# A spectral mixer with a feed-forward layer on one core: transfers of the prologue begun by another engine, weight stores and some loads at other steps

## The chip, the core and the metric

The kernel runs on one core of one Trainium2 chip. The time is the device time of one execution in microseconds; three runs of the kernel before have a median of 2681.63 us. TensorE does matmuls, ScalarE (ACT) copies, casts and activations, VectorE (DVE) and GpSimd (POOL) elementwise work, and SyncE (SP) begins transfers. Each engine works through its own instructions in order, so a waiting instruction holds all that stand behind it on that engine.

## The reference

For each of 8 sequences `x` of 3072 tokens by 256 channels: a real Fourier transform along the sequence, a complex matmul of each frequency with `w_r`, `w_i` (256 x 256), a bias, soft shrinkage by 0.01, and the inverse transform. Then a feed-forward layer on all 24576 tokens: `h = x @ w_in` (256 to 2048), softplus, `@ w_out` (2048 to 256). In short:

```
X = rfft(x, axis=1)
Yr = Xr @ w_r - Xi @ w_i + b_r ;  Yi = Xr @ w_i + Xi @ w_r + b_i
Y = sign(Y) * max(|Y| - 0.01, 0)         (for both parts)
out = softplus(irfft(Y) @ w_in) @ w_out
```

Inputs and output are float32.

## The kernel before

The transform of a sequence is done in stages of small dense matmuls, with 3072 = 96 x 32. `s1` multiplies 16 chunks of x by a 96 x 96 matrix and gives `a`; `s3` does the second factor on 12 pairs of groups (`ap` tiles, with their matrix `g1`); `mix` multiplies by `w_r` and `w_i`, adds the bias and shrinks; `s4` gives `d`; `s5` gives the 512-token blocks of the layer's input (`dp` tiles of d, with their matrix `hm`). From a stage to the next the partitions change, so `a` and `d` are written to DRAM (`a_dr`, `d_dr`) and read back; for the first sequence (b = 0) `a` stays in `a0` in SBUF and `ap` is copied from there (line 273). The `d` loads of a sequence wait until all 12 stores of `d` have landed.

The feed-forward layer takes tokens in pairs of 512 and the hidden units in 8 blocks of 256, with a seven-product scheme for a block (`slot_products`, banks "c" and "e" of PSUM). Matmuls are done in split precision: an operand becomes a high and a low part, and `mm3` (lines 207 to 210) does three matmuls. The layer's weights come as 64-bit floats. `split_w` (line 146) takes one block through a chain of ScalarE, VectorE and GpSimd work, one part a step, to a tile `w` of high and low parts, which is stored to DRAM (line 195, `w_dr`). The main loop reads the blocks back with `stream_w` (line 200), 896 KB for a block of `w_in` and 512 KB for one of `w_out`, two buffers each. The tile `w` is `w_1` for `w_in` blocks of the prologue, else `wp`, which has one buffer (line 168). Blocks are started three steps apart after the prologue; in a block's third part VectorE writes `w` for the first time (L178 or L182), in its fourth ScalarE makes the high half (L192), in its fifth VectorE the low half (L194).

The order of the work is written out by hand. A step has a number; steps below 0 are the prologue (`t0` = -66), each key of the main loop (a pair of 512-token blocks and one hidden block) has four. In a step come, in this order: the feed-forward products of the step, the due parts of `split_w` (the dictionary `before`), at most one product of the transform (`steps`), the loads and splits asked for at this step (`fill`, in the order in which they were asked for), what was put off in the step before (`later`, stores of `a` and `d` among it), and the second half of the feed-forward work. Each engine gets its instructions in this order. `early` is a list that is emptied at step -1; up to there it tells the prologue. In the prologue `s1` uses four tiles of `a1` in turn for `a` of b = 1 (line 257), and `d` has two.

All transfers of the prologue but a few constants are begun by SP: x (line 231), the weights as they come (line 143), `g1` (line 749, `g1_0` for b = 0), `ap` (line 273), stores of `a` and `d` (line 100), stores of weights (line 195), their loads (line 204), `hm` and `dp` (lines 440, 441). `plan_s1` (line 645) asks for x of chunk c seven steps before its product. For the chunks 10 to 15 of b = 1 x has two buffers (line 230), so a load of x c waits for the split of x c-2.

Of the kernel before, what the change touches and what calls it, by code (L numbers as in the profile page):

```python
# [10 lines left out]
F32 = mybir.dt.float32  # L11
# [8 lines left out]
NG = 24  # L20
# [13 lines left out]
def tile_spectral_mixer_mlp(ctx, tc, x, w_r, w_i, bias, bias_0, w_in, w_out, f, f_hi, f_lo, g1, g3, g3_hi, g3_lo, hm, out):  # L34
# [12 lines left out]
    nc = tc.nc  # L47
# [21 lines left out]
    a0 = sb.tile([P, N2 * D], F32, tag="y0", name="a0", bufs=1)[:N1].rearrange("p (n c) -> p n c", n=N2)  # L69
# [5 lines left out]
    w1_dr = [dram.tile([P, 2 * 7 * P], F32, name=f"w1_dr{m2}", tag=f"w1_dr{m2}", bufs=1) for m2 in range(NM // 2)]  # L75
    w2_dr = [dram.tile([P, 2 * 2 * D], F32, name=f"w2_dr{m2}", tag=f"w2_dr{m2}", bufs=1) for m2 in range(NM // 2)]
# [19 lines left out]

    def store(dst, src, what):

        def start():
            nc.sync.dma_start(dst, src)  # L100
            stored[what] += 1

        later.append(start)
# [42 lines left out]
    def split_w(which, m2):  # L146

        st = stages.pop((which, m2)).bitcast(U32).rearrange("p (n w) -> p n w", w=2)
        lw, hw = st[:, :, 0], st[:, :, 1]
        t = sb.tile([P, 512], F32, tag="t", name="wt", bufs=5)
        u = sb.tile([P, 512], F32, tag="ot", name="wu")
        ti, ui = t.bitcast(U32), u.bitcast(U32)
        v, g = nc.vector, nc.gpsimd
        nc.scalar.activation(u, hw.bitcast(F32), AF.Square)
        v.tensor_scalar(out=ti, in0=hw, scalar1=3, scalar2=0x3FFFFFF8, op0=ALU.logical_shift_left, op1=ALU.bitwise_and)
        v.scalar_tensor_tensor(out=ti, in0=hw, scalar=0xC0000000, in1=ti, op0=ALU.bitwise_and, op1=ALU.bitwise_or)  # L160
        nc.scalar.mul(lw.bitcast(F32), lw, 2.0 ** -52)
        yield
        v.scalar_tensor_tensor(out=t, in0=u, scalar=2.0 ** -30, in1=t, op0=ALU.is_ge, op1=ALU.mult)
        v.tensor_scalar(out=ui, in0=ti, scalar1=0xFF800000, scalar2=None, op0=ALU.bitwise_and)
        g.tensor_tensor(out=u, in0=lw.bitcast(F32), in1=u, op=ALU.mult)
        yield
        n = 7 * P if which else 2 * D
        w = w_1 if early and which else sb.tile([P, 2 * 7 * P], F32R, tag="wp", name="wp", bufs=1)
        w = w[:, :2 * n]
        hi, lo, src = w[:, :n], w[:, n:], w[:, n:].bitcast(F32)  # L170
        ahead = bool(early)
        e = g if ahead else v
        if which:

            tm, um = [a.rearrange("p (k m n) -> p m k n", k=2, m=2) for a in (t, u)]
            a21 = tm[:, 1, 0]
            o = [src[:, i * P:(i + 1) * P] for i in range(7)]
            e.tensor_tensor(out=src[:, A11 * P:(A11 + 2) * P].rearrange("p (k n) -> p k n", k=2), in0=tm[:, 0], in1=um[:, 0], op=ALU.add)  # L178
            e.tensor_tensor(out=a21, in0=a21, in1=um[:, 1, 0], op=ALU.add)
            e.tensor_tensor(out=o[A22], in0=tm[:, 1, 1], in1=um[:, 1, 1], op=ALU.add)  # L180
        else:
            e.tensor_tensor(out=src, in0=t, in1=u, op=ALU.add)  # L182
        if ahead:
            yield
            yield
        if which:
            v.tensor_tensor(out=o[S1], in0=a21, in1=o[A22], op=ALU.add)
            v.tensor_tensor(out=o[S3], in0=o[A11], in1=a21, op=ALU.subtract)
            v.tensor_tensor(out=o[S2], in0=o[S1], in1=o[A11], op=ALU.subtract)
            v.tensor_tensor(out=o[S4], in0=o[A12], in1=o[S2], op=ALU.subtract)  # L190
        yield
        nc.scalar.copy(hi, src)  # L192
        yield
        v.tensor_tensor(out=lo, in0=src, in1=hi.bitcast(F32), op=ALU.subtract)  # L194
        nc.sync.dma_start((w1_dr if which else w2_dr)[m2][:, :], w.bitcast(F32))
        stored["w", which, m2] += 1

    w_t = {}
# [22 lines left out]
    early = [None]  # L221
# [44 lines left out]
    def load_a(b, gp):  # L266
        assert stored["a", b] == 16
        t = sb.tile([P, 512 + 2 * P], F32, tag="ap", name="ap", bufs=3)
        t, g1_t = t[:, :512].rearrange("p (g c) -> p g c", g=2), t[:, 512:].rearrange("p (g n) -> p g n", g=2)
        if b == 0:  # L270
            g1_t = g1_0[:, 2 * gp:2 * gp + 2]
            for g in range(2):
                nc.sync.dma_start(t[:, g, :], a0[2 * gp + g::NG])
        else:
            nc.sync.dma_start(g1_t, g1[:, 2 * gp:2 * gp + 2])
            nc.sync.dma_start(t, a_dr[b][8 * gp:8 * gp + 8].rearrange("(g q) n c -> (q n) g c", g=2))
        a_sb[b, gp] = t, g1_t
# [301 lines left out]
    def slot_products(s, key, prev):  # L579

        if s == 0:
            if key:
                ffn1(key, "c", A11, B11)
                ffn1(key, "e", A12, B21)
                snap(key, C11, "c")
            if prev:
                softplus(prev, C21)
                high(prev, C21)
                low(prev, C12)
            if key:  # L590
                add(key, C11, "e")
            if prev:
                low(prev, C21)
        elif s == 1 and key:
            ffn1(key, "c", S2, T2, start=False)
            ffn1(key, "e", S3, T3)
            softplus(key, C11)
            high(key, C11)
            snap(key, C21, "c")
            low(key, C11)  # L600
        elif s == 2 and key:
            ffn1(key, "c", S1, T1, start=False)
            snap(key, C22, "c")
            add(key, C22, "e")
        elif s == 3 and key:
            ffn1(key, "c", S4, B22, start=False)
            ffn1(key, "e", A22, T4, start=False)
            softplus(key, C22)
            high(key, C22)
            softplus(key, C12, "c")  # L610
            high(key, C12)
            low(key, C22)
            add(key, C21, "e")

    def slot_second(s, key, prev):
        if s < 3:
            if prev:
                what = (C22, C12, C21)[s]
                ffn2(prev, what, what == C22 and prev[2] == 0, what != C22 and prev[2] == NM // 2 - 1)
                if s == 2:  # L620
                    del w_t[0, prev]
        elif key:
            ffn2(key, C11, key[2] == 0, False)
            del w_t[1, key]


    with tc.manual_schedule():
# [3 lines left out]
        fill, steps, before = {}, {}, {}  # L631
# [3 lines left out]
        def at(i, f, *args):  # L635
            fill.setdefault(int(i), []).append((f, args))

        def product(i, f, *args):
            i = int(i)
            while i in steps:  # L640
                i += 1
            steps[i] = f, args
            return i

        def plan_s1(b, start, step, first=0):
            for c in range(first, 16):
                t = product(start + step * (c - first), s1, b, c)
                at(t - 3, split_x, b, c)
                at(t - 7, load_x, b, c)

        def plan_mix(b, start, step):
            mixed = done = start
# [29 lines left out]
        t0 = -len(first)  # L682
        for t, (what, b, i) in enumerate(first, t0):
# [9 lines left out]
                product(t, s4, b, i)  # L693
            else:
                product(t, s5, 0, b, i)
        for t, i, j in ((t0 + 15, 0, 4), (t0 + 16, 4, 12), (t0 + 22, 12, NG)):
            at(t, nc.sync.dma_start, g1_0[:, i:j], g1[:, i:j])
        at(t0 + 18, nc.sync.dma_start, bias0, bias_0)
        at(-6, nc.sync.dma_start, bias_sb, bias)
# [3 lines left out]
        for j in range(NM):  # L703
            t = t0 + 23 + 5 * j if j < 9 else 1 + 3 * (j - 9)
            at(t - (6 if j < 9 else 4 if j < 12 else 2), load_w, (j + 1) % 2, j // 2)
            before.setdefault(t, []).append(split_w((j + 1) % 2, j // 2))
# [9 lines left out]

        nt = NT
        plan_s1(1, 1, 1.6, 10)
        for b in range(B):
            for bp in range(1, NPAIR):  # L720
# [15 lines left out]
        for i in range(min([*fill, *steps]), nt * B + 3):  # L736
            due = len(later)
            if i >= 0:
                g, s = divmod(i, 4)
                key, prev = keys[g], keys[g - 1] if g else None  # L740
                slot_products(s, key, prev)
            for part in before.pop(i, ()):
                if next(part, part) is None:
                    before.setdefault(i + 1, []).append(part)
            if i in steps:
                f, args = steps.pop(i)
                f(*args)
            for f, args in fill.pop(i, ()):
                f(*args)
            for _ in range(due):  # L750
                later.popleft()()
            if i >= 0:
                slot_second(s, key, prev)
# [101 lines left out]
```

## Time and profile before

| | us |
|---|---|
| median of three runs | 2681.63 |
| lowest and highest run | 2677.0, 2682.29 |
| span of the profiled execution | 2678.0 |
| TensorE busy in it | 2603.8 (97%) |
| VectorE busy | 1626.2 (61%) |
| ScalarE busy | 1719.5 (64%) |
| GpSimd busy | 301.3 (11%) |

The page gives the span of the profiled execution, from its first to its last instruction, and no time around it; the median of the runs is 3.6 us above this span. Busy time is an average over stages: the table says that TensorE is nearly full over the whole, and not where it waits. That is read from windows and timelines of the first 250 us, in which the prologue and the conversion of the weights lie.

### The profile page before, as it was taken

Reading aid. Unit: us, or ns where it says so; the run is one execution under the profiler, and the core shown is the slowest. Engines: PE = TensorE matmul, PEld = TensorE weight load, DVE = VectorE, ACT = ScalarE, POOL = GpSimd, SP = SyncE. Lnnn points to the kernel's source line nnn. Section 1 sums busy time; section 2 is a strip of 40 time slices with the busy share of each in tenths; the row PEclk is TensorE's granted clock in tenths of the full one; section 3 lists DMA queues with packets and bytes.
Section 4 is the critical chain, followed back from the end, with each engine's and each line's share of the span. In section 5 each row is a group of like instructions: output and inputs, shape, how many; then the busy total and the mean of one; then the engine's idle time right before and its main releaser. Section 6 shows DMA issues by size and latency. Waiting matters only on the chain.

```text
span 2678.0 us, 36264 instructions
## 1 busy us (share of the span) xinstructions
PE 2603.8 (97%) x13059; PEld 2184.2 (82%) x13059; DVE 1626.2 (61%) x2701; ACT 1719.5 (64%) x3115; POOL 301.3 (11%) x292
## 2 busy tenths in 40 slices
PE   7768999999999999999999999999999999999999
PEld 5546888888888888888888888888888888888887
DVE  3666665666646666566665666556665666645454
ACT  3365666666666666666676666666666666666665
POOL 2432110110101101101011011010010000000000
PEclk8889999999999999999999999999999999999999
DMA  6766556556455565564555644646455455445543
GB/s 191 254 210 206 194 164 198 166 187 193 157 188 178 178 198 170 179 205 156 184 172 172 217 159 153 220 163 198 164 167 191 155 170 188 142 154 183 186 147 110
DMA packets 186116, 479.73 MB, mean 179 GB/s; under 512 B 18097, under 2 KB 86961, under 8 KB 185937
## 3 DMA queue, kind: packets, MB, share of 16 engines
q1 hardware_dynamic: 185376, 476.95, 55.1%
q8 instruction: 103, 1.69, 0.3%
q0 software_dynamic: 560, 0.47, 0.1%
q14 instruction: 77, 0.62, 0.1%
HBM read 390.31 MB, written 83.89 MB: 177 GB/s over the span
## 4 chain that ended last, share of the span: by engine, by line
PE 88%; DVE 2%; DMA 2%; ACT 1%; issue 0%; POOL 0%; SPq 0%; DVEq 0%; ACTq 0%; POOLq 0%
PE pso L208 13%; PE pso L209 12%; PE pso L210 12%; PE psc L208 6%; PE psc L210 6%; PE psc L209 6%; PE pse L208 5%; PE pse L210 5%; PE pse L209 5%; PE psf L455 4%; PE psf L209 4%; PE psf L208 4%; PE psf L210 4%; PE psf L287 2%; DMA w_dr<-wp 1%; DVE shrunk L413 0%
## 5 line engine op out<-in xcount | busy, mean ns | idle before, releaser
L553 DVE TENSOR_TENSOR gl<-t,gh 128x512 fp32r<-128x512 f32 x768 | 533.2, 694 | 349.7 <-ACT gh L547 346.8
L532 ACT COPY t<-psc 128x512 f32<-128x512 f32 x576 | 337.0, 585 | 504.4 <-PE psc L210 502.4
L537 DVE TENSOR_TENSOR t<-pse,t 128x512 f32<-128x512 f32 x576 | 396.2, 688 | 426.9 <-ACT t L532 278.3
L208 PE MATMUL pso<-gh,w 128*128 128x512 f32 x1536 | 616.2, 401 | 0.0
L209 PE MATMUL pso<-gl,w 128*128 128x512 f32 x1536 | 600.0, 391 | 0.0
L210 PE MATMUL pso<-gh,w 128*128 128x512 f32 x1536 | 599.5, 390 | 0.0
L547 ACT CAST gh<-t 128x512 fp32r<-128x512 f32 x768 | 476.8, 621 | 58.2 <-PE pso L210 34.4
L543 ACT ACTIVATE t<-t 128x512 f32<-128x512 f32 x576 | 364.5, 633 | 58.7 <-DVE t L537 58.0
L210 PEld LDWEIGHTS pso<-gh,w 128*128 128x128 f32 x1536 | 288.7, 188 | 62.5
L208 PEld LDWEIGHTS pso<-gh,w 128*128 128x128 f32 x1536 | 290.1, 189 | 54.9
L209 PEld LDWEIGHTS pso<-gl,w 128*128 128x128 f32 x1536 | 290.0, 189 | 51.4
L208 PE MATMUL psc<-y_sb,w 128*128 128x512 f32 x768 | 301.6, 393 | 16.1 <-DMA w<-w_dr 7.8
L210 PE MATMUL psc<-y_sb,w 128*128 128x512 f32 x768 | 300.1, 391 | 0.0
L209 PE MATMUL psc<-y_sb,w 128*128 128x512 f32 x768 | 299.6, 390 | 0.0
L208 PE MATMUL pse<-y_sb,w 128*128 128x512 f32 x576 | 227.8, 396 | 14.4 <-DVE t L537 7.9
L115 POOL TENSOR_TENSOR xl<-xt,xh 96x512 fp32r<-96x512 f32 x102 | 134.1, 1317 | 938.3 <-ACT xh L106 783.6
L209 PE MATMUL pse<-y_sb,w 128*128 128x512 f32 x576 | 225.2, 391 | 0.0
L210 PE MATMUL pse<-y_sb,w 128*128 128x512 f32 x576 | 225.1, 391 | 0.0
L489 POOL TENSOR_TENSOR y_sb<-raw,y_sb 128x512 fp32r<-128x512 f32 x69 | 92.3, 1337 | 1128.5 <-ACT y_sb L486 1124.9
L208 PEld LDWEIGHTS psc<-y_sb,w 128*128 128x128 f32 x768 | 144.5, 188 | 51.0 <-ACT t L532 10.2
L210 PEld LDWEIGHTS psc<-y_sb,w 128*128 128x128 f32 x768 | 144.6, 188 | 31.0
L209 PEld LDWEIGHTS psc<-y_sb,w 128*128 128x128 f32 x768 | 144.6, 188 | 29.7
(131 smaller groups left out, 3637.8 us busy)
## 6 DMA issues: line engine op xcount, KB each, us to landing
w<-w_dr SPq DMA_DIRECT2D x192, 896.0 KB
w<-w_dr SPq DMA_DIRECT2D x192, 512.0 KB
dp<-d_dr SPq DMA_DIRECT2D x80, 384.0 KB
xt<-in_x SPq DMA_DIRECT2D x128, 192.0 KB
d_dr<-d SPq DMA_DIRECT2D x96, 256.0 KB
out_y<-ot SPq DMA_DIRECT2D x96, 256.0 KB
ap<-a_dr SPq DMA_DIRECT2D x84, 256.0 KB
a_dr<-a SPq DMA_DIRECT2D x102, 192.0 KB
```

Source lines behind the costliest of these rows:

```text
L115: (eng or nc.vector).tensor_tensor(out=lo, in0=src, in1=hi.bitcast(F32), op=ALU.subtract)
L208: nc.tensor.matmul(ps, wh, xh, start=start, stop=False, skip_group_check=more)
L209: nc.tensor.matmul(ps, wh, xl, start=False, stop=False, skip_group_check=more)
L210: nc.tensor.matmul(ps, wl, xh, start=False, stop=stop, skip_group_check=more)
L287: nc.tensor.matmul(xv[:, g, k], t[:, g, k * P:(k + 1) * P], g1_t[:, g].rearrange("p (c s) -> p c s", c=2), start=True, stop=True,)
L455: nc.tensor.matmul(ps[:, t - blk * BLK:t - blk * BLK + n], d_sb[b, blk // 2, n2 // 4][0][:, n2 % 4, k * P:(k + 1) * P], d_sb[b, blk // 2, ...
L489: eng.tensor_tensor(out=lo, in0=raw[j], in1=hi.bitcast(F32), op=ALU.subtract)
L532: nc.scalar.copy(t, banks[bank])
L537: nc.vector.tensor_tensor(out=t, in0=banks[bank], in1=t, op=ALU.add)
L543: nc.scalar.activation(t, banks[bank] if bank else t, AF.Softplus)
L547: nc.scalar.copy(gh, ct[key, what])
L553: nc.vector.tensor_tensor(out=gl, in0=ct.pop((key, what)), in1=gh.bitcast(F32), op=ALU.subtract)
```

## The change

Six edits. While `early` is not empty, stores of `a` and `d` are begun by ScalarE. Weight stores come one step later than the low half, and blocks whose third part lies in the prologue (`ahead`) are stored by ScalarE. The first three pairs of `ap` of b = 0 (six transfers) are begun by ScalarE. The loads of x for b = 1, chunks 10 to 15, are asked for five steps ahead of the product and not seven. The first part of `g1_0` is asked for at `t0 + 9` and not at `t0 + 15`. Where several weight blocks have a part in the same step, those under way now come ahead of one that starts in it, in their old order; before, they were appended behind it.

```diff
@@ store
+        queue = nc.scalar if early else nc.sync
+
         def start():
-            nc.sync.dma_start(dst, src)
+            queue.dma_start(dst, src)
             stored[what] += 1
@@ split_w
         v.tensor_tensor(out=lo, in0=src, in1=hi.bitcast(F32), op=ALU.subtract)
-        nc.sync.dma_start((w1_dr if which else w2_dr)[m2][:, :], w.bitcast(F32))
+        yield
+        (nc.scalar if ahead else nc.sync).dma_start((w1_dr if which else w2_dr)[m2][:, :], w.bitcast(F32))
@@ load_a
             for g in range(2):
-                nc.sync.dma_start(t[:, g, :], a0[2 * gp + g::NG])
+                (nc.scalar if gp < 3 else nc.sync).dma_start(t[:, g, :], a0[2 * gp + g::NG])
@@ plan_s1
                 at(t - 3, split_x, b, c)
-                at(t - 7, load_x, b, c)
+                at(t - (5 if b == 1 else 7), load_x, b, c)
@@ the plan of the prologue
-        for t, i, j in ((t0 + 15, 0, 4), (t0 + 16, 4, 12), (t0 + 22, 12, NG)):
+        for t, i, j in ((t0 + 9, 0, 4), (t0 + 16, 4, 12), (t0 + 22, 12, NG)):
             at(t, nc.sync.dma_start, g1_0[:, i:j], g1[:, i:j])
@@ the loop over steps
-            for part in before.pop(i, ()):
-                if next(part, part) is None:
-                    before.setdefault(i + 1, []).append(part)
+            left = [part for part in before.pop(i, ()) if next(part, part) is None]
+            if left:
+                before[i + 1] = left + before.get(i + 1, [])
```

## Rows read from the trace of the kernel before

**Rows 1.** Windows: us, busy us (and count) of five engines, TensorE clock, DMA share, GB/s.
```profile
75.00:108.00 33.00, 26.70 (x156) 20.84 (x157) 28.98 (x43) 12.01 (x24) 19.62 (x15) 0.94 0.79 263
108.00:125.00 17.00, 10.37 (x31) 6.19 (x29) 4.13 (x9) 4.37 (x8) 6.37 (x8) 0.70 1.00 289
200.00:250.00 50.00, 38.23 (x180) 31.46 (x181) 30.20 (x56) 24.49 (x46) 10.42 (x13) 0.90 0.65 211
400.00:600.00 200.00, 199.21 (x1021) 168.46 (x1019) 121.06 (x202) 134.44 (x245) 25.34 (x27) 1.00 0.59 186
...
205.00:225.00 20.00, 14.87 (x63) 11.35 (x61) 8.03 (x14) 7.15 (x13) 5.08 (x11) 0.91 1.02 314
```

**Rows 2.** Timeline of TensorE: start, duration, line, tiles; in brackets idle before and releaser.
```profile
27.83 2.53 PE L287 MATMUL psf<-y,ap 128*128 128x128 f32 x8 [4.25 <-DMA ap<-a]
...
43.41 0.58 PE L210 MATMUL psf<-wmh,w 128*128 128x256 f32 x1 [4.77 <-DVE w L115]
...
119.88 1.99 PE L455 MATMUL psf<-dp 96*128 96x96 f32 x8 [5.95 <-DMA dp<-d_dr]
...
139.20 0.79 PE L208 MATMUL pse<-y_sb,w 128*128 128x512 f32 x1 [6.50 <-ACT y_sb L474]
...
157.72 0.77 PE L208 MATMUL psc<-y_sb,w 128*128 128x512 f32 x1 [7.14 <-DMA w<-w_dr]
```

**Rows 3.** Timeline of SP's queue; two answers have the starts at 20.84.
```profile
20.84 7.17 SPq L273 DMA_DIRECT2D ap<-a  x6
...
20.84 1.34 SPq L273 DMA_DIRECT2D ap<-a  x2
...
118.11 1.33 SPq L100 DMA_DIRECT2D a_dr<-y  x2
...
143.02 0.31 SPq L231 DMA_DIRECT2D xt<-in_x  x1
...
152.77 0.42 SPq L204 DMA_DIRECT2D w<-w_dr  x1
...
193.02 0.33 SPq L195 DMA_DIRECT2D w_dr<-wp  x1
194.15 0.39 SPq L143 DMA_DIRECT2D w<-in_w_out  x1
...
203.89 0.32 SPq L195 DMA_DIRECT2D w_dr<-wp  x1
205.04 0.38 SPq L143 DMA_DIRECT2D w<-in_w_in  x1
```

**Rows 4.** Timeline of ScalarE, its copies of a, w and y_sb.
```profile
21.90 0.58 ACT L260 COPY y<-psf 96x512 f32<-96x512 f32 x1 [0.28 <-PE psf L249]
...
30.40 0.58 ACT L301 CAST w<-psf 128x512 fp32r<-128x512 f32 x1 [4.74 <-PE psf L287]
...
108.25 0.58 ACT L260 COPY y<-psf 96x512 f32<-96x512 f32 x1
...
125.88 0.58 ACT L260 COPY y<-psf 96x512 f32<-96x512 f32 x1 [12.38 <-DMA a_dr<-y]
...
138.57 0.57 ACT L474 CAST y_sb<-psf 128x512 fp32r<-128x512 f32 x1
```

**Rows 5.** Timeline of VectorE.
```profile
41.52 0.69 DVE L380 TENSOR_TENSOR z<-psf,bias 128x512 f32<-128x512 f32 x1 [9.19 <-DMA bias<-in_bias]
...
195.85 0.43 DVE L178 TENSOR_TENSOR wp<-wt,wu 128x256 f32<-128x256 f32 x1
...
201.07 0.69 DVE L537 TENSOR_TENSOR t<-pse,t 128x512 f32<-128x512 f32 x1 [1.68 <-ACT t L532]
...
207.85 0.69 DVE L182 TENSOR_TENSOR wp<-wt,wu 128x512 f32<-128x512 f32 x1 [1.70 <-DMA w_dr<-wp]
...
214.07 0.69 DVE L553 TENSOR_TENSOR gl<-t,gh 128x512 fp32r<-128x512 f32 x1 [2.21 <-ACT gh L547]
...
225.40 0.42 DVE L178 TENSOR_TENSOR wp<-wt,wu 128x256 f32<-128x256 f32 x1 [8.37 <-DMA w_dr<-wp]
```

## The prediction, made before the changed kernel ran

> **What bounds the kernel now.** I read the windows first. From 400 us on TensorE works 199.2 of 200 us [rows 1]: whatever the change does there is covered by matmuls. It works 26.7 of 33 us from 75 to 108, 10.4 of 17 from 108 to 125 and 38.2 of 50 from 200 to 250 [rows 1]. All edits fall before step 24, so the prologue (below 141 us) and the 25 steps after it (to 250 us) decide. Then TensorE's timeline says what each gap waits for [rows 2]: 4.25 us for the first ap, 4.77 for VectorE's low half, 5.95 for dp, 6.50 for a copy on ScalarE, 7.14 for the first weights of the second pass over the hidden blocks. The queues of SP, ScalarE and VectorE [rows 3 to 5] tell why.
>
> **Loads of x at other steps (b = 1), and with them the 7.14 us.** A tile of x c is free when c-2 has been split. Before, x14 stands in step 0 ahead of the weight load, and SP waits for x12's split of step 2; only at 152.77 the load starts that TensorE gets at 157.72 [rows 2, 3]. Now x14 is in step 2 and x13 in step 0; x13 was begun at 143.02 [rows 3]. The load can start about 143.5 and, with the same 4.95 us to its use (157.72 - 152.77), is there at 148.4. TensorE would want it at 157.72 - 7.14 = 150.58. The stall goes, -7.1 us; what is late next is VectorE. At worst it uses the gap to catch up and takes 2 us of it back, so -5.1 to -7.1. The other x are still there a step before their split: cost 0.
>
> **Stores of a on ScalarE's queue, and with them the 6.50 us.** In steps 56 to 61 four a tiles take turns. The fifth copy waits for the first store's landing and runs at 125.88, after 12.38 us idle [rows 4]. On SP that store stands behind the d loads, which wait for all stores of d: it started at 118.11 [rows 3], though its copy ran at 108.25 [rows 4]. ScalarE is in order, so its copy of B21 came at 138.57 [rows 4] and TensorE's matmul at 139.20 [rows 2]. Now ScalarE begins the store itself, a step (some 2 us) after the copy, about 111; with the 7.8 us that it took (118.11 to 125.88) it lands at 119, and the copy runs 7 us earlier. What is late next is TensorE's own s5, which ends about 131. I take the whole 6.50: -6.5. SP is also held no more by weight stores, so it asks for the weight loads of steps 53 to 57 (1.9 MB) before the last d stores rather than beside them, and the 5.95 us for dp could shrink too: up to -12.4. But a stores now run beside the d loads, and in this stretch the DMA share is 1.00 [rows 1]: if these lose what the copies gain, 0.
>
> The Trainium skill (DMA: Bandwidth & Descriptors, section "Issuing engines are not separate DMA queues") speaks against this edit: transfers started by any engine run on the same 16 DMA engines and interleave, and starting them elsewhere saves only the time on the sequencer. The share of 1.00 [rows 1] agrees; the 12.38 us of rows 4 are, however, a wait of SP's order and not of the engines. By the rule alone this term would be 0 and the sum 6.5 us higher; it is the second rival's ground.
>
> **First six ap and the prologue's other starts on ScalarE.** On SP six starts of ap took 7.17 us, 1.2 each [rows 3]. ScalarE reaches them after the second b = 1 copy (21.90 + 0.58 = 22.5 [rows 4]), 1.7 us later than SP at 20.84; but SP's queue ahead of them is shorter by the first g1 load, now six steps earlier. I leave the 4.25 us as they are (-1 to +2). Behind them ScalarE has three a starts at 0.67 (118.11: two in 1.33 [rows 3]), two copies and two casts at some 0.6 each, then the copy of 30.40 [rows 4]. At the pace of SP's first two ap, 0.67 each (two in 1.34 [rows 3]), 22.5 + 4.0 + 2.0 + 2.4 = 30.9, a loss of 0.5; at 1.2, 34.1, of 3.7. The gain: VectorE waited 9.19 us for the bias until 41.52 [rows 5], which stood on SP behind eight ap and an a store; that gave the 4.77 us. It still stands behind the fourth ap pair, and one us of the 4.77 stays (the low half comes after z in VectorE's order). I take -1.0 with that loss in it, from +3.7 to -3.8. The later ap loads and d copies, less held by SP, gain 0: from 75 to 108 VectorE works 29.0 of 33 us and sets the pace [rows 1] (its 4.0 idle are the most that can go). The d and weight starts cost ScalarE 0.3 to 0.7 us each [rows 3], beside 12.0 us of work in those 33 and 4.4 in the 17 after [rows 1]: 0.
>
> **Weight stores a step later.** This is the term that costs. wp has one buffer: the next weight's first write (VectorE L178 or L182, two steps after its start, starts three steps apart) waits for the store's landing. Before, the store went out in the step of its low half, ahead of that step's loads; now it stands behind them, in the step of the next write. What the row shows when such a store lands late: VectorE stood 8.37 us at 225.40 [rows 5]. Stores in order after step 0:
> - w_out 4, step 5 to 6: nothing between. w_in 5, 8 to 9: two loads, whose buffers TensorE frees a step before the low half is ready. w_in 7, 20 to 21: the same. 0 each.
> - w_out 5, 11 to 12: before at 193.02, landed by 195.85 (no wait there) [rows 3, 5]: 0.52 MB in 2.8 us; at 314 GB/s [rows 1] 1.7 of it are data, 1.2 the rest. Now the stage load is ahead (before at 194.15; it waits for GpSimd, whose input VectorE now makes after the low half, +0.7, so 194.8), an ap load of 0.39 MB and a weight load of 0.52. With these, 1.97 MB at 314 GB/s are 6.3 us: landed at 194.8 + 6.3 + 1.2 = 202.3, a wait of 6.5. VectorE had 1.68 us idle behind it at 201.07 [rows 5]: +4.8.
> - w_in 6, 14 to 15: before at 203.89, the write waited 1.70 at 207.85 [rows 3, 5]. Now behind the stage load (before at 205.04; + 0.7 + 4.8 = 210.5) and four d chunks with their hm: 2.69 MB, and 0.92 of its own, 3.6 MB, 11.5 us at the full rate of this stretch (share 1.02 [rows 1]). Landed at 223.2; the write is ready at 207.85 - 1.70 + 4.8 = 210.95: a wait of 12.3, 10.6 more; less the 2.21 idle at 214.07 [rows 5], +8.4.
> - w_out 6, 17 to 18: it waited 8.37 before, since those same loads were ahead; now they are gone and one load and one ap are ahead: 0.
>
> Together +13.2. Bounds: 0, if VectorE is not what the PE waits for there (TensorE ran 38.2 of 50 us [rows 1], so some slack is there), and 18.8 without any slack.
>
> **The sum.** -7.1 - 6.5 - 1.0 + 13.2 = -1.4 us. The profiled span is 2678.0; the page gives no time around it, and the median of three runs, 2681.63, lies 3.6 above, 0.14%. So 2676.6 of span, 2680 measured. From 250 us on nothing gives it back: TensorE is full [rows 1].
>
> **The rivals.** (1) Faster: the late stores bind less. For it: at 195.85 VectorE did not wait at all, and TensorE can run ffn blocks ahead of VectorE there. Against: 8.37 us at 225.40 show that it stands when a store is late, and the share is 1.02. With only 3 of the 13.2: 2678.0 - 11.6 = 2666.4, measured 2670. It decides if the two waits together stay under 5 us.
> (2) Slower: ScalarE, now a queue of its own in front of its copies. Place: 22 to 36 and 108 to 125 us. Price: the 3.7 us of the ap starts, no 6.5 and no 1.0. It decides once a start on ScalarE takes 1.2 us rather than 0.67, or an a store beside the d loads lands later than 126. Then -7.1 + 13.2 + 3.7 = +9.8: 2691. For it: 1.2 each on SP, the share of 1.00. Against: ScalarE's queue begins empty. By the rule named above, with starts at 0.67, it would be -1.4 + 6.5 = +5.1, measured 2687.
> (3) The edits cancel because the same transfers end at the same times: 2682.
>
> **How the numbers follow.** 0.2%, 5.4 us, is what a measurement of this kernel can tell: 2676.3 to 2687.0 counts as the same. Forecast 0.42, own range 2675 to 2686: of it 0.09 are faster and 0.05 slower. Rival 1 0.26, rival 2 0.27, rival 3 0.05. Faster 0.35, same 0.33, slower 0.32. The range takes in rival 1 and most of rival 2 with the bounds: 2665 to 2694.
>
> **What would show it.** Right: no wait of TensorE for a weight load about step 4; ScalarE's long wait for a_dr in the prologue gone and the matmul of B21 within 2 us of its copy with no gap of 6 us before; VectorE's waits at L178 and L182 for w_dr over 6 and over 10 us at steps 12 and 15, where they were 0 and 1.7. Wrong: those waits under 3 us (rival 1); ScalarE's first copy of w after the ap starts later than 33 us, or a wait for a_dr as long as before (rival 2). If TensorE has new gaps past 250 us, the prediction is wrong in its ground.

## The result: 0.6% slower, and where the trace after shows it

| | median us | before, beside it | ratio, 95% interval |
|---|---|---|---|
| the changed kernel | 2696.18 (2694.69 to 2697.34) | 2680.65 | 1.0060, 1.0048 to 1.0072 |

Predicted were 2680 us and no measurable difference, with a range to 2694: wrong. The changed kernel is 15.5 us slower; the span of its profiled execution is 2695.6 us, 17.6 more than before. The windows of the changed kernel, with the columns of [rows 1], say in which stretch:

```profile
75.00:108.00 33.00, 25.76 (x158) 21.23 (x157) 31.68 (x48) 14.44 (x27) 16.90 (x14) 0.95 0.84 277
108.00:125.00 17.00, 10.03 (x32) 5.82 (x30) 5.95 (x13) 7.27 (x13) 6.94 (x9) 0.76 0.83 260
200.00:250.00 50.00, 27.23 (x102) 22.03 (x101) 20.32 (x43) 17.44 (x31) 6.04 (x11) 0.67 0.56 184
400.00:600.00 200.00, 198.56 (x1004) 167.22 (x1003) 120.68 (x202) 134.15 (x246) 20.83 (x23) 1.00 0.60 190
...
220.00:225.00 5.00, 0.00 (x0) 0.00 (x0) 0.00 (x0) 0.00 (x0) 0.00 (x0) 0.50 1.03 341
225.00:230.00 5.00, 1.54 (x4) 1.26 (x5) 3.79 (x7) 3.07 (x6) 0.92 (x4) 0.50 0.61 253
```

From 200 to 250 us TensorE works 27.2 us, where [rows 1] had 38.2; for five of them no engine computes and only transfers run (share 1.03). From 400 us on it is as full as before. The granted clock over the 50 us is 0.67, 0.90 before: after standing, TensorE resumes at 0.50, which is the lower of its two levels (1.2 of 2.4 GHz).

TensorE's timeline of the changed kernel, beside [rows 2]:

```profile
28.12 2.49 PE L290 MATMUL psf<-y,ap 128*128 128x128 f32 x8 [4.78 <-DMA ap<-a]
...
38.82 0.58 PE L211 MATMUL psf<-wmh,w 128*128 128x256 f32 x1 [5.50 <-ACT w L304]
...
118.24 1.99 PE L458 MATMUL psf<-dp 96*128 96x96 f32 x8 [4.62 <-ACT y L263]
...
128.01 6.58 PE L458 MATMUL psf<-dp 96*128 96x96 f32 x30 [4.31 <-DMA dp<-d_dr]
137.86 0.80 PE L211 MATMUL pse<-y_sb,w 128*128 128x512 f32 x1 [1.83 <-ACT y_sb L477]
...
149.89 0.50 PE L211 MATMUL psc<-y_sb,w 128*128 128x512 f32 x1 [0.46 <-ACT t L546]
...
162.85 0.80 PE L211 MATMUL psc<-y_sb,w 128*128 128x512 f32 x1 [4.69 <-ACT t L535]
...
228.46 0.79 PE L211 MATMUL pse<-y_sb,w 128*128 128x512 f32 x1 [11.77 <-DVE t L540]
```

TensorE does the same 13059 matmuls in the same order, so the n-th of one trace can be set beside the n-th of the other. The one of 139.20 in [rows 2] comes 1.3 us earlier (137.86). The one of 157.72 comes 7.8 us earlier (149.89), and the 7.14 us wait for weights is gone. By 162.85 the lead is 3.9 us, at 194.4 it is 3.5, at 199.5 us 0.9. At 216.3 it is 6.7 us late, and then TensorE stands 11.77 us for VectorE; the matmul of 228.46 ran at 210.14 before, so it is 18.3 us late. From there to the last matmul the distance stays between 15.7 and 20.0 us: the whole loss arises between 194 and 229 us.

What VectorE stood for is in its timeline, beside [rows 5]:

```profile
44.93 0.69 DVE L383 TENSOR_TENSOR z<-psf,bias 128x512 f32<-128x512 f32 x1 [4.83 <-PE psf L213]
...
202.00 0.42 DVE L180 TENSOR_TENSOR wp<-wt,wu 128x256 f32<-128x256 f32 x1 [9.13 <-DMA w_dr<-wp]
206.99 0.69 DVE L540 TENSOR_TENSOR t<-pse,t 128x512 f32<-128x512 f32 x1 [1.44 <-ACT t L535]
226.17 0.69 DVE L184 TENSOR_TENSOR wp<-wt,wu 128x512 f32<-128x512 f32 x1 [13.84 <-DMA w_dr<-wp]
...
227.72 0.68 DVE L540 TENSOR_TENSOR t<-pse,t 128x512 f32<-128x512 f32 x1
...
243.28 0.42 DVE L180 TENSOR_TENSOR wp<-wt,wu 128x256 f32<-128x256 f32 x1 [8.40 <-DMA w_dr<-wp]
```

The waits for `w_dr<-wp` were 0, 1.70 and 8.37 us in [rows 5]; they are 9.13, 13.84 and 8.40. The addition at 227.72, on which TensorE's 11.77 us end, is queued three instructions behind the write of 226.17. SP's queue, beside [rows 3], has the cause:

```profile
151.26 0.33 SPq L234 DMA_DIRECT2D xt<-in_x  x1
151.64 0.69 SPq L102 DMA_DIRECT2D a_dr<-a  x1
...
194.29 0.42 SPq L198 DMA_DIRECT2D w_dr<-wp  x1
...
211.21 0.38 SPq L145 DMA_DIRECT2D w<-in_w_in  x1
...
215.40 0.46 SPq L444 DMA_DIRECT2D dp<-d_dr  x1
215.96 0.51 SPq L198 DMA_DIRECT2D w_dr<-wp  x1
```

The store of w_in 6 is begun at 215.96, behind the stage load of 211.21 and four d chunks with their `hm`. In [rows 3] it stood ahead of that load. It lands at 226.17, ten us after its start.

### The profile page after: what moved, and what is told of

Read it like the earlier page. It is cut to its first block, busy times and chain, and to the rows that moved or that the text cites. A ratio compares the mean times of both kernels' runs of the same rounds, so it can differ in the third digit from the quotient of the medians.

```text
span 2695.6 us, 36257 instructions
## 1 busy us (share of the span) xinstructions
PE 2609.2 (97%) x13059; PEld 2189.3 (81%) x13059; DVE 1626.4 (60%) x2701; ACT 1720.6 (64%) x3115; POOL 296.1 (11%) x292
## 4 chain that ended last, share of the span: by engine, by line
PE 87%; DVE 2%; DMA 2%; ACT 2%; issue 0%; SPq 0%; POOL 0%; DVEq 0%; ACTq 0%; POOLq 0%
PE pso L211 12%; PE pso L212 12%; PE pso L213 12%; PE psc L211 6%; PE psc L213 6%; PE psc L212 6%; PE pse L211 5%; PE pse L213 5%; PE pse L212 5%; PE psf L458 4%; PE psf L212 4%; PE psf L211 4%; PE psf L213 4%; PE psf L290 2%; DMA w_dr<-wp 1%; DVE shrunk L416 1%
```

## The experiments

Times are medians; each difference is to the runs of the kernel before on the same chip. Diffs are against the kernel that the line names.

| run | median us | difference | ratio, 95% interval |
|---|---|---|---|
| e1 changed, weight stores in their old step | 2675.82 | -4.7 | 0.9982, 0.9973 to 0.9992 |
| e2 before, weight stores a step later | 2699.86 | +19.4 | 1.0073, 1.0058 to 1.0088 |
| e3 before, x loads | 2677.23 | -3.3 | 0.9988, 0.9978 to 0.9997 |
| e4 before, ScalarE's starts | 2684.67 | +4.2 | 1.0017, 1.0008 to 1.0027 |
| e5 changed, later store only in the prologue | 2674.49 | -6.4 | 0.9976, 0.9966 to 0.9986 |
| e6 as e2, d loads behind the store of w_in 6 | 2693.66 | +12.8 | 1.0043, 1.0029 to 1.0057 |
| e7 as e4, ap on SP | 2688.68 | +7.8 | 1.0028, 1.0017 to 1.0038 |
| e8 as e3, all a stores of b = 1 by ScalarE | 2682.16 | +1.3 | 1.0003, 0.9993 to 1.0012 |
| e9 as e3, a stores 4 to 9 by ScalarE | 2678.19 | -3.1 | 0.9991, 0.9983 to 1.0000 |
| e10 as e5, first ap and a stores 0 to 3 on SP | 2675.27 | -6.0 | 0.9981, 0.9973 to 0.9990 |
| e11 as e2, w_in 6 in its own step | 2688.63 | +7.3 | 1.0035, 1.0022 to 1.0048 |
| e12 as e5, a stores 4 to 9 on SP | 2675.31 | -6.0 | 0.9980, 0.9971 to 0.9989 |
| e13 as e9, those stores by GpSimd | 2674.54 | -6.0 | 0.9979, 0.9970 to 0.9988 |
| e14 as e5, a stores 4 to 9 by GpSimd | 2673.26 | -7.3 | 0.9973, 0.9962 to 0.9984 |
| e15 as e5, a stores 0 to 3 by GpSimd | 2672.65 | -7.9 | 0.9971, 0.9961 to 0.9981 |
| e16 as e5, all prologue a stores by GpSimd | 2673.32 | -7.2 | 0.9974, 0.9964 to 0.9984 |

**The late weight stores: e1, e2, e5, e6, e11.** e1 is the changed kernel without the added step:

```diff
         v.tensor_tensor(out=lo, in0=src, in1=hi.bitcast(F32), op=ALU.subtract)
-        yield
```

> The changed kernel with one part undone: each weight store goes out in the step of its low half again (by ScalarE for the blocks ahead, by SP for the others); everything else stays. Theory A (the late stores, whose landing VectorE waits for at 170, 202 and 226 us, make the loss): the waits of 3.98, 9.13 and 13.84 us fall to 0 to 3 us each, and the time falls by 18 to 24 us, to 2672 to 2678. Theory B (ScalarE, held by its own starts of transfers, makes it, and the later stalls only show what would be late anyway): 2688 to 2696.

e2 is the kernel before with that step and the new order of the parts:

```diff
+        yield
         nc.sync.dma_start((w1_dr if which else w2_dr)[m2][:, :], w.bitcast(F32))
```

> The kernel before with only the weight stores a step later (all by SP) and the parts under way put first. Theory A: VectorE waits for w_dr at steps 12 and 15 as in the changed kernel, and the time rises by 14 to 24 us, to 2695 to 2705. Theory B: within 5 us of before, 2676 to 2686.

Undone, the step takes 20.2 us off the changed kernel (15.5 + 4.7, each beside its own runs of before); put into the kernel before, together with the new order of the parts, it adds 19.4. So this one edit is more than the whole loss, and the other five together gain about 5 (e1). The new order without the step was not tried. In e6 the four d chunks that stand ahead of the store of w_in 6 are asked for a step later, so they come behind it:

```diff
-at(start - (3 if (b, bp) == (1, 0) else 4), load_d, b, bp, c)
+at(start - (3 if (b, bp) in ((1, 0), (0, 1)) else 4), load_d, b, bp, c)
```

> The kernel before with all weight stores a step later by SP (the run of that alone took 2699.9), and with the loads of d for the second pair of blocks a step later too, so that they stand behind the store of w_in block 6 and not ahead of it. Theory A3 (the 2.1 MB of d ahead of the store are what VectorE waits for at 228 us): the wait of 13.72 us falls under 5 and the time falls by 7 to 11 us, to 2689 to 2693. Rival A4 (the later store itself costs, whatever is ahead of it; or the d chunks, now later, stop TensorE at s5 instead): 2697 to 2701.

e11 leaves that one store in its own step:

```diff
-            yield
+        if (which, m2) != (1, 6):
+            yield
```

> The kernel before with the weight stores a step later, all but that of w_in 6, which stays in its own step. Theory (each late store holds VectorE and that goes to the end whole): of the 19.4 us that all late stores cost, the 12 us by which the wait at step 15 was lengthened go, 2688 us, with waits of some 8 us at step 12 and under 2 at step 15. Rival (VectorE's stands overlap with what it would wait for anyway): 2694 us or more, since other waits grow in their place.

VectorE's two stands at steps 12 and 15, first in e2, then in e6, then the one that e11 keeps:

```profile
204.05 0.43 DVE L178 TENSOR_TENSOR wp<-wt,wu 128x256 f32<-128x256 f32 x1 [8.20 <-DMA w_dr<-wp]
...
228.10 0.69 DVE L182 TENSOR_TENSOR wp<-wt,wu 128x512 f32<-128x512 f32 x1 [13.72 <-DMA w_dr<-wp]
```

```profile
205.09 0.43 DVE L178 TENSOR_TENSOR wp<-wt,wu 128x256 f32<-128x256 f32 x1 [8.58 <-DMA w_dr<-wp]
...
221.09 0.69 DVE L182 TENSOR_TENSOR wp<-wt,wu 128x512 f32<-128x512 f32 x1 [5.66 <-DMA w_dr<-wp]
```

```profile
202.46 0.43 DVE L178 TENSOR_TENSOR wp<-wt,wu 128x256 f32<-128x256 f32 x1 [8.29 <-DMA w_dr<-wp]
```

In e2 the wait at step 15 is 12.0 us longer than the 1.70 of [rows 5], and e11, without it, is 12.0 us nearer to its kernel before: the wait goes to the end whole. e6 shortens it by 8.1 and gains 6.6 by the same comparison, just short of its first theory in both (5.66 us for under 5, 2693.7 for 2693): the place in the queue is the cause, though some comes back elsewhere. e11's rest of 7.3 us goes with the 8.29 at step 12; in its trace 2.7 us of it come at w_out 6, whose wait there is 11.44 and not 8.37.

e5 keeps the later store for the blocks of the prologue, where ScalarE begins it:

```diff
-        yield
+        if ahead:
+            yield
```

> The changed kernel, with the weight stores a step later only for the blocks ahead, which ScalarE stores; the others, stored by SP, go out in the step of their low half as before. Theory A1 (a step later helps where ScalarE starts the store, since ScalarE then does not stand until VectorE has the low half; it costs where SP's loads get ahead): 2671 to 2674, some 3 us under the run with all stores in the step of their low half, and the matmuls at 90 us no longer 4 us late. Rival A2 (the step makes no difference to ScalarE): as that run, 2674 to 2678.

It beats both kernels, at a time in the range of rival A2. Against e1 (all stores in their own step) its 1.7 us lie inside the intervals: in the prologue no cost or gain of the step can be told.

**The x loads: e3.** The kernel before with `t - (5 if b == 1 else 7)` alone.

> The kernel before with only the loads of x for b = 1 asked for five steps ahead. The wait of 7.14 us for the weights of the second hidden block goes under all theories. As predicted: -7 us, 2673.5. Rival (seen in the changed kernel: ScalarE waits 4.36 us for a store of a at 160 that SP began late, behind a load of x): 3 to 5 us come back there, so 2676 to 2679.

The matmul of 157.72 in [rows 2] comes 8.6 us earlier and its wait is gone, as predicted, but only 3.3 us are left at the end (0.8 to 5.9 by the interval; in the profiled execution 2.5 us of lead are there at the matmul of 139.20 already). ScalarE's timeline in e3 shows where the rest went:

```profile
155.72 0.58 ACT L260 COPY a<-psf 96x512 f32<-96x512 f32 x1 [2.21 <-DMA a_dr<-a]
164.25 0.58 ACT L260 COPY a<-psf 96x512 f32<-96x512 f32 x1 [5.76 <-DMA a_dr<-a]
```

Past the prologue two tiles take turns for a, so a copy waits until the store of the copy before last has landed. In the kernel before only the second of these two copies waited, 3.36 us at 168.83. ScalarE's next copy for TensorE stands behind it: TensorE waits 4.50 us at 165.37, where it waited 1.01. SP begins the first of these stores behind an x load for which it waits, in the kernel before and then in e3:

```profile
152.40 0.31 SPq L231 DMA_DIRECT2D xt<-in_x  x1
...
155.17 0.60 SPq L100 DMA_DIRECT2D a_dr<-a  x1
```

```profile
150.50 0.33 SPq L231 DMA_DIRECT2D xt<-in_x  x1
150.88 0.60 SPq L100 DMA_DIRECT2D a_dr<-a  x1
```

So SP's wait stood in front of the stores before as well. In e3 the store is 4.3 us earlier, but TensorE is 8.6 us earlier, and the copies reach their tiles too soon. In the changed kernel it is the same: the x load at 151.26 above, the store at 151.64, a wait of ScalarE of 4.36 us at 160.03, TensorE's 4.69 us at 162.85.

**ScalarE's starts: e4, e7, e8.** e4 has all the starts by ScalarE and the earlier first g1, with old steps for the rest; e7 is e4 with ap and g1 as before, so only stores moved:

```diff
-                (nc.scalar if gp < 3 else nc.sync).dma_start(t[:, g, :], a0[2 * gp + g::NG])
+                nc.sync.dma_start(t[:, g, :], a0[2 * gp + g::NG])
```

> The kernel before with only the starts on ScalarE (stores of a and d, the first six ap, stores of the weights ahead, in the step of their low half) and the earlier first load of g1. As predicted: ScalarE's wait for a_dr goes and the time falls by 6 to 8 us, to 2673 to 2675. Theory B: the first mix starts 5 us late as in the changed kernel and the d chunks land no earlier, so +3 to +9, 2684 to 2690. Between them, what the changed kernel's matmuls show when they are set beside the same ones of before (1.3 us ahead at the first pse): 2679.

> Only the stores of a, d and of the weights ahead are begun by ScalarE (in the step of the low half); the first ap and the first load of g1 are SP's and in their old steps. Theory B1 (the six ap on ScalarE, and the a stores that share their completion semaphores, hold ScalarE until 38 us, but VectorE makes this up by 50 us): within 2 us of the run with the ap too, 2682 to 2686. Rival B2 (the ap are the loss): 2674 to 2679, the first mix at 33 and not at 39 us, and the lead kept.

e8 is e3 with every a store of b = 1 begun by ScalarE, those past the prologue too:

```diff
+        queue = nc.scalar if what == ("a", 1) else nc.sync
```

> The kernel before with two edits: x of b = 1 asked for five steps ahead, and all stores of a for b = 1 (and no others) begun by ScalarE. Theory C1 (the 12.4 us wait for a_dr in the prologue and the 4 to 6 us wait for it near step 4 are both waits of SP's order): -7 for the weights, -4 to -7 for the 6.5 us stall: 2667 to 2671. Rival C2 (the d chunks lose in the shared queues what the copies gain): 2673 to 2677, as with the x loads alone or a little less.

Moving starts alone is a loss of 4.2 us, as theory B of e4 said, and of 7.8 without the ap. e7 and e8 both lie above all that was expected of them. TensorE in e7:

```profile
32.22 1.22 PE L289 MATMUL psf<-y,ap 128*128 128x128 f32 x4 [2.66 <-DMA ap<-a]
36.23 1.20 PE L289 MATMUL psf<-y,ap 128*128 128x128 f32 x4 [2.79 <-DMA ap<-a]
```

The first a stores, begun by ScalarE while SP is still at ap, delay them; with the ap ahead of the stores on ScalarE this does not happen (e4). At 50 us e7 is 5.0 us behind the kernel before, and e4 only 1.0; e4 loses its time later and is 7.4 us behind at 90 us, and what holds it there was not tried. In e8 both gaps are there too, and VectorE waits 8.12 us for a weight store at 175.63 (2.48 in e3). So e8 keeps nothing of e3's gain.

**The a stores of chunks 4 to 9: e9, e12, and e10.** These carry the term of -6.5. e9 is e3 with them by ScalarE; e12 is e5 with them back on SP; e10 is e5 with the other part, ap, the first g1 and a stores 0 to 3, back on SP.

```diff
-..., ("a", b))
+..., ("a", b), nc.scalar if early and c > 3 else nc.sync)
```

> The kernel before with x of b = 1 asked for five steps ahead and, alone of the other edits, the six prologue stores of a (b = 1, chunks 4 to 9) begun by ScalarE; ap, first a stores, d, g1 and weights stay with SP in their old steps. Theory (the stores' data share the engines with the d loads, so the copies gain and the dp chunks lose): the stores bring about 1 of the 6.5 us that I predicted, and the x loads their measured 3.3: 2676 us. Rival (the whole 6.5 is there once the first ap are left alone): 2671 us, with the dp gap at 5.95 and no 6.5 us behind it.

> The changed kernel with the later store only for the blocks of the prologue (2674.5 us), and with the a stores of chunks 4 to 9 back on SP. Theory (that edit is worth about 1 us here): 2675 to 2676 us, ScalarE's wait for a_dr back near 12 us but the dp chunks earlier. Rival (it is worth the 6.5 that I predicted, and the loss lies elsewhere): 2681 us.

> The changed kernel with the later store only for the blocks of the prologue (2674.5 us), and with the first six ap, the first g1 and the a stores of chunks 0 to 3 back on SP in their old steps. Theory (the 5.6 us that the first mix comes late are made up by 50 us, so this edit is worth nothing): 2674 to 2676 us, first mix near 33.3 us, and the same times from 50 us on. Rival (ScalarE's starts at the head cost what is not made up): 2670 us.

All three came out nearest to the first theory (e9 at 2678, where it said 2676): neither edit is worth anything that can be measured (e9 against e3, e10 and e12 against e5, each within 0.5 us). TensorE in e3, then in e9:

```profile
116.71 2.00 PE L455 MATMUL psf<-dp 96*128 96x96 f32 x8 [6.23 <-DMA dp<-d_dr]
...
136.72 0.80 PE L208 MATMUL pse<-y_sb,w 128*128 128x512 f32 x1 [7.15 <-ACT y_sb L474]
```

```profile
120.83 2.00 PE L457 MATMUL psf<-dp 96*128 96x96 f32 x8 [8.71 <-DMA dp<-d_dr]
...
127.84 6.58 PE L457 MATMUL psf<-dp 96*128 96x96 f32 x30 [1.12 <-DMA dp<-d_dr]
137.69 0.80 PE L210 MATMUL pse<-y_sb,w 128*128 128x512 f32 x1 [1.84 <-ACT y_sb L476]
```

The gap of 7.15 us shrinks to 1.84, but the d chunks, on which `s5` works just before, come 4.1 and later 6.2 us later: what the copies gain the loads lose.

**Why the d loads come later: e13 to e16.** Two causes fitted. Either the stores' data take the DMA engines from the loads, or SP's starts of the loads are held. The waits of SP's queue in e9 between 105 and 126 us (who waits, for what, us in total, times, longest) speak for the second:

```profile
SPq L442 <- DMA a_dr<-y: 3.5, 1, 3.5
SPq L443 <- DMA w<-w_dr: 2.8, 1, 2.8
```

A load of `hm` into a `dp` tile waits for a store of a, with which it shares no data. In the records of the starts the transfers of SP and ScalarE take eight completion semaphores in turn; this `hm` has the one that ScalarE's a store of 110.70 used, eight transfers before, and is begun when that has landed (121.29 and 121.36). The wait of 2.8 us is of the same kind, for a weight load that SP itself began eight transfers before. Transfers begun by GpSimd have other semaphores. So e13 and e14 are e9 and e12 with the six stores begun by GpSimd, e15 has the first four there, e16 all ten.

```diff
-nc.scalar if early and c > 3 else nc.sync)
+nc.gpsimd if early and c > 3 else nc.sync)
```

> As e9 (the kernel before with x of b = 1 five steps ahead), but the six a stores of chunks 4 to 9 are begun by GpSimd, whose starts use other completion semaphores than those of SP and ScalarE. Theory (in e9 the starts of the d loads on SP were held until a stores had landed that used the same semaphore): the dp chunks come as in e3 (first matmul on them 116 to 118 us, second gap under 1 us), the copies early, and the 7.15 us gap before the first pse matmul shrinks to 2: 2672 us. Rival (the stores' data take the engines from the d loads): dp as late as in e9, 2677 us.

> As e12 (changed kernel, later store only for the prologue's blocks), with the six a stores of chunks 4 to 9 begun by GpSimd. Theory of the held starts: dp as in e12 or earlier, no gap of 4 us at the third chunk, pse matmul 4 to 5 us earlier than in e5: 2670 us. Rival of the shared engines: 2675 us as e5 and e12.

> The changed kernel with the later store only for the prologue's blocks, and the a stores of chunks 0 to 3 begun by GpSimd. In e5 the third of them held ScalarE's cast 6.56 us at its head. Theory (its start waited for the first store's landing on the same semaphore): the wait is gone, cast of the first s3 near 33 us, first mix 5 us earlier; by 50 us both are level, so the time stays 2674.5. Rival (the cast is held by the transfers of ap and a themselves): the cast stays near 40 us.

> e14 and e15 together: all ten prologue stores of a by GpSimd, the rest as in e5. Theory of the held starts: 2670 us, as e14. Rival of the shared engines: 2675 us.

TensorE in e13:

```profile
118.43 2.00 PE L457 MATMUL psf<-dp 96*128 96x96 f32 x8 [7.76 <-DMA dp<-d_dr]
121.52 8.72 PE L457 MATMUL psf<-dp 96*128 96x96 f32 x40 [1.09 <-DMA dp<-d_dr]
133.55 0.80 PE L210 MATMUL pse<-y_sb,w 128*128 128x512 f32 x1 [1.88 <-ACT y_sb L476]
```

No wait of SP for `a_dr<-y` is left. The chunks come 2.4 to 4.1 us earlier than in e9, though the first is still 1.7 later than in e3, and the pse matmul comes at 133.55, 4.1 us before e9's. Beside its own kernel before, e13 gains 6.0 us and e9 3.1; the intervals just overlap (0.9970 to 0.9988 and 0.9983 to 1.0000), and 2674.5 lies between what the two theories expected. So the held starts are shown in the trace. With them go 2.4 of the 4.1 us by which the first chunk is late in e9, and 4.1 of the later 6.2; the rest may be transfers that run at the same time, and whether GpSimd's starts differ in more than their semaphores was not tried. In e14 the pse matmul is 2.4 us before e12's, but of that 0.6 are left at the last matmul; its time is not to be told from e12's. e14 and e16, both at 2673.3, lie between the 2670 and the 2675 us that were expected. e15 shows the start that held ScalarE: the cast after the first `s3` waits for TensorE and no more for `a_dr`, and the first mix, at 40.62 us in e5, runs at 35.93. I expected no gain in time from it; 2672.65 us is the best of all medians, but its 1.5 us to e5, each beside its own runs of before, lie inside the intervals.

## Why the prediction was wrong, step by step

**The weight stores a step later: +13.2 predicted, +19.4 (e2) and +20.2 (e1) measured.** This step failed by its size; the mechanism, the blocks (w_out 5 and w_in 6) and the engines were right. The waits were to be 6.5 and 12.3 us and are 8.2 and 13.7 in e2; w_out 6 kept its wait, as predicted (8.37 before, 8.22 in e2). What failed first is the deduction of VectorE's idle behind each wait, 1.68 and 2.21 us [rows 5], as slack. Behind the first wait the idle comes back, 1.44 us at 206.99 above, after a wait of 9.13. ScalarE's timeline of the changed kernel says why:

```profile
203.92 0.94 ACT L194 CAST wp<-wp 128x896 fp32r<-128x896 f32 x1 [10.36 <-DVE wp L192]
...
206.39 0.57 ACT L535 COPY t<-psc 128x512 f32<-128x512 f32 x1
```

VectorE's idle is a wait for this copy, and TensorE waits 2.89 us for the same copy before its matmul of 207.01. The copy stands in ScalarE's queue behind the cast of the high half, which waits for VectorE's late write. So the late store holds what ends the idle too, and the idle is no slack.

In e2 the distance of the same matmuls to before goes from -0.5 to +8.4 over the stand of 8.20, and from there to +20.3 over the one that is 12.0 longer. Behind the second stand TensorE is idle 12.02 us, before its matmul of 230.38. Behind the first it is idle only 4.72 us, before its matmul of 209.06, so TensorE did have some slack; but the 44 matmuls from 200.3 to 218.0 us take 12.9 us beside that idle, where they took 9.2. The granted clock is 0.72 from 200 to 218 us, and the kernel before ran the same matmuls at 1.00. That the first stand too goes to the end at its full size is thus a sum of two parts, and the prediction had neither. The bound "0, if VectorE is not what the PE waits for there" was excluded by these stands. The upper bound without slack, 18.8, was nearly the answer, but it counts the 1.70 us that the second wait had before; without them it is 6.5 + 10.6 = 17.1. The rest is queueing: in e2 the store of w_out 5 lands 8.7 us after the first transfer of its group starts (195.32), and I had 7.5.

**The x loads: -7.1 predicted, -3.3 alone (e3).** The stall went as written, but "what is late next" was named wrongly. It was not VectorE but ScalarE's copies of a, which wait for stores: in e3 the first of these begins 4.3 us earlier, where TensorE comes 8.6 us earlier. I had followed the load and its user, and not which transfers the engines reach next once the stall is gone.

**The a stores: -6.5 predicted, 0 measured (e9, e12).** Here the zero bound ("if these lose what the copies gain") was the answer. ScalarE's timeline of the changed kernel, beside [rows 4]:

```profile
21.72 6.59 ACTq L276 DMA_DIRECT2D ap<-a  x6
...
29.48 0.58 ACT L263 COPY y<-psf 96x512 f32<-96x512 f32 x1 [7.25 <-DMA ap<-a]
...
37.55 0.59 ACTq L102 DMA_DIRECT2D a_dr<-y  x1
38.18 0.58 ACT L304 CAST w<-psf 128x512 fp32r<-128x512 f32 x1 [6.55 <-DMA a_dr<-y]
...
122.10 0.58 ACT L263 COPY y<-psf 96x512 f32<-96x512 f32 x1 [4.78 <-DMA a_dr<-y]
```

The wait of 12.38 us is 4.78, and the copy 3.8 us earlier (122.10 for 125.88). But `s5` did not end at 131: it waited 4.31 us for the third chunk and ended at 134.6 (128.01 + 6.58).

The Trainium skill (DMA: Bandwidth & Descriptors, section "Issuing engines are not separate DMA queues") says that a transfer started by another engine runs on the same 16 DMA engines and saves only the start. It made this term 0, and 0 it was. Its remark that the saving is usually small does not cover what the runs show beside it: moving starts alone cost 4.2 to 7.8 us (e4, e7), and the same stores begun by GpSimd put the pse matmul 4.1 us earlier than begun by ScalarE (e13 against e9).

**The first ap: -1.0 predicted, 0 measured (e10 against e5).** The ScalarE side of rival 2 came true at its place: six starts of ap took 6.59 us (1.1 each), and the third a store held the cast until 38.18, where [rows 4] have 30.40. Its price of 3.7 us did not reach the end: the first mix is 5.6 us late (38.82), and at 50 us TensorE is 0.9 behind; VectorE's `z` now waits for its matmuls (44.93 above) and no more for the bias.

**The sum.** The terms were -7.1 - 6.5 - 1.0 + 13.2 = -1.4. With what e3, e9, e10 and e2 measured for each they are -3.3 + 0 + 0 + 19.4 = +16; measured is +15.5. That they meet so closely is partly luck: the intervals of e2 and e3 are 4.0 and 2.5 us wide to either side, and the terms don't add everywhere: e4's starts alone cost 4.2 us, and e1, which is e4 with the x loads and the new order of the parts, is 4.7 below before. What each of these two is worth on top of e4 was not tried.

**The rivals.** The sign of rival 2 was right, and its time, 2691, nearest, but not its mechanism: it had the 13.2 in it as I did, and let ScalarE's starts make the difference. Rival 1 (late stores bind less) is refuted, rival 3 too. As written, the ground held: past 250 us nothing is lost or given back.

## What to carry to other kernels

Before a start is moved down a queue, write out what stands between its old and its new place, its bytes, and who reuses its buffer; then charge the whole wait. Take off idle as slack only where what ends it does not stand behind the same late transfer, on whatever engine, and count what the matmuls cost at the lower clock after a stand. When a stall is taken away, look for the transfers that the engines reach next, and whether they come earlier too. Starts of two engines can be tied together by the completion semaphores that they share, so a store on another queue can hold a load that has nothing to do with it.

## What the runs showed that I had not expected

A start can hold its engine for a transfer of unrelated data. In the changed kernel ScalarE's third a store had the semaphore of the first, begun at 28.40, and was itself begun at 37.55; ScalarE's cast behind it was idle for 6.55 us. In e4 and e5 the same row has 6.71 and 6.56, and in e15, where GpSimd begins these stores, the wait is gone.
